# Chunk attention and two MLPs on one core: another order for the attention units, loads and weight pieces of the first stage

## The chip, the cores and the metric

One core of a Trainium2 chip. Its engines run side by side, each through its own list of instructions in order: TensorE (PE; its weight loads are listed as PEld), VectorE (DVE), ScalarE (ACT), GpSimd (POOL) and SyncE (SP). An engine waits for another only through semaphores. SP and POOL issue the DMAs here. The metric is the device time of one execution in microseconds (us); smaller is better.

## The reference

```python
# q, k, v: (4, 8, 576, 64) float32; attention inside chunks of 64 positions
scores = (q_c @ k_c.T) / sqrt(64);  attn = softmax(scores);  out = attn @ v_c
x = out.transpose(0, 2, 1, 3).reshape(2304, 512)
# first MLP:  d_ff 1536
y = ((x @ w_a) * (x @ w_b)) @ w_out
# second MLP: d_ff 2048, g a rational function of h
h = y @ w_in
g = (a0 + a1 h + a2 h^2 + a3 h^3) / (1 + |b0||h| + |b1| h^2 + 1e-6)
return g @ w_out2                               # (2304, 512) float32
```

## The kernel before

**Products.** The large products are made from pairs of fp32r tiles, a high part (`hi`) and the rest (`lo`). `mm3` (lines 250 to 254) adds three products into one bank: weight hi by x hi, weight hi by x lo, weight lo by x hi. So the first product needs the hi parts, the second x lo, the third weight lo.

**Tokens and units.** The 2304 tokens are 18 units of 128. The attention of a unit u is a list of pieces, each named by a letter: `k` and `q` (four transposes on PE into a PSUM tile, then a copy on ACT), `S` (scores: 32 small matmul instructions on PE into the two PSUM banks "a" and "b", then two maxima and two subtractions on DVE), `X` (exp on ACT), `E` (sum, reciprocal, product on DVE), `P` (four transposes on PE, a copy on ACT), `V` (32 small matmul instructions on PE, then two casts to x hi on ACT), `L` (two subtractions on DVE, to x lo). Units 0 to 2 are the first 384 tokens, units 3 to 5 the next 384. The later units are done in pairs (`a_pair`), whose S, V and transposes use the same PSUM tiles. `ps_at`, for k, q and P, has two tiles; "a" and "b" are shared by S and V.

**Weight pieces.** Each 128 x 1024 raw weight tile is made into its hi and lo parts in four pieces (`w_piece`, lines 201 to 236), a `w` in the lists: piece 0 is two ACT instructions, piece 1 writes the hi of the tile before (ACT) and shifts (DVE), piece 2 is one ACT instruction and writes the lo of the tile before (DVE, line 199) and fetches a raw tile into a buffer that is now free, piece 3 is a DVE add (line 234) and a store. So the lo part of tile n is there once piece 2 of tile n + 1 has run. Tiles are numbered in the order a0, b0, a1, b1, ... of the blocks i of the first MLP.

**Start.** The loads are issued in the order of `LOADS`, all on SP's queue. Then `FIRST` writes out by hand the order in which units 0 to 2 and the first 15 weight pieces are issued; `dN` is N idle products of the identity (`warm`), two PE instructions each; `+k5` issues the load of unit 5's k.

**First stage.** `seq` then runs over (i, h), h being the half of 384 tokens: blocks 0 to 3 with h = 0, blocks 0 to 3 with h = 1, then the other blocks with both. `ab_half` makes one 128 x 384 tile of x @ w_a or x @ w_b from 12 products. In its middle and at its end `half()` is called: it brings the weight pieces up to a count (`w_until`), then moves a clock of its own, `now`, on by 0.5 (`tick`) and issues every piece in `todo` whose time has come, by time and then by the order in which it was put in. So a piece with time t is issued after half number n = 2t - 1. This text writes A0 for the tile of block 0 with w_a, B0 with w_b, and so on; A0 to B3 with h = 0 are sixteen halves, and A0 with h = 1, which reads units 3 to 5, begins at t = 8.

```python
for n in range(UH):                                          # units 3, 4, 5
    a_unit(UH + n, 1.0 + 0.5 * n, (0, 0.5, 1.5, 2, 2.5, 4, 5))    # k q S X E P V
FROM, PER, GAP = 5.5, 4.5, 3.0                               # start of the pairs
w_until(min(12 + 2 * n, 32) / 4 if n < 17 else (n + 18) / 4)
```

So units 3, 4 and 5 are half a unit of time apart: k at 1.0, 1.5 and 2.0, S at 2.5, 3.0 and 3.5, E at 3.5, 4.0 and 4.5, P at 5.0, 5.5 and 6.0, V at 6.0, 6.5 and 7.0. The six pairs follow from 5.5, one every 4.5, the last three another 3.0 later. After the last unit of a group of six, `x_second` puts 14 sums, casts and subtractions of x into `todo`. The stages behind (the first MLP on the other tokens by a scheme with fewer products, its second product, the second MLP) are not touched.

Of the kernel before, what the change touches and what calls it, by code (L numbers as in the profile page):

```python
# [20 lines left out]
def chunk_attention_two_mlps(  # L21
# [35 lines left out]
    P = 128  # L57
    B, H, S, D = q.shape
# [16 lines left out]
    UH = GH // P  # L75
    NQ = NT // GT

    FIRST = (  # L80
        "k0 d2 q0 w w S0 w X0 k1 d2 w E0 q1 w S1 X1 P0 w k2 q2 E1 V0 w S2 X2 L0 P1 w +k5 +q5 w V1 d4 E2 w w +v3 +v4 +v5 "
        "L1 d2 P2 d4 w w V2 d4 L2 w w"
    ).split()
    LOADS = "k0 q0 w k1 q1 v0 w k2 q2 v1 w v2 w k3 q3 k4 q4".split()

    AHEAD = 4
    NWP = 12 - AHEAD
# [150 lines left out]
    def w_until(tiles):  # L238

        while n_cv[1] < min(4 * tiles, 4 * n_cv[2]):  # L240
            w_piece()
# [18 lines left out]
    todo = []  # L260
    now = [0.0]

    def later(dt, f):
        todo.append((now[0] + dt, n_todo[0], f))
        n_todo[0] += 1

    n_todo = [0]
# [13 lines left out]
    un = {}  # L281
# [46 lines left out]
    def a_transpose(u, nm):  # L328

        t = raw.pop((nm, u)).rearrange("p (a b) d -> p a (b d)", b=2)  # L330
        pool, tag = (ps_acc, "acc") if u < UH else (ps_at, "at")
        ps = pool.tile([P, HP, P], F32, name="at", tag=tag)
        for hp in range(HP):
            nc.tensor.transpose(ps[:, hp, :], t[:, hp, :], ident)
        o = a_tmp(u, nm + "T") if u < 2 * UH else a_both(u, nm + "T")[:, u % 2]
        nc.scalar.copy(o, ps)
        un[nm + "T", u] = o

    def a_scores(u):

        qT, kT = un.pop(("qT", u)), un.pop(("kT", u))
        ps = [ps_ab.tile([P, HP, CH], F32, name="at", tag=tag) for tag in "ab"]
        for a in range(2):
            for c in range(2):
                for t in range(2):
                    for b in range(2):
                        r, half, cols = (slice(n * CH, (n + 1) * CH) for n in (b, t, c))
                        hp = 2 * a + t  # L350
                        nc.tensor.matmul(
                            ps[b][half, 2 * a + c, :], qT[r, hp, cols], kT[r, hp, cols], start=True, stop=True
                        )
        m = p_e.tile([P, 2, HP], F32, name="m", tag="m")
        e = a_tmp(u, "e").rearrange("p x (y d) -> p (x y) d", d=CH).rearrange("p (b x) d -> p b x d", b=2)
        for b in range(2):
            nc.vector.tensor_reduce(m[:, b], ps[b], AX.X, ALU.max)
        for b in range(2):
            nc.vector.tensor_tensor(
                e[:, b], ps[b], m[:, b].unsqueeze(2).to_broadcast([P, HP, CH]), ALU.subtract  # L360
            )
        un["e", u] = e.rearrange("p b x d -> p (b x) d")

    def a_exp(u):
        nc.scalar.activation(un["e", u], un["e", u], AF.Exp, scale=SCALE)

    def a_soft(u):
        e = un["e", u]
        s = p_e.tile([P, H], F32, name="s", tag="s")
        nc.vector.tensor_reduce(s, e, AX.X, ALU.add)  # L370
        nc.vector.tensor_scalar(s, s, 1e-9, None, ALU.add)
        nc.vector.reciprocal(s, s)
        nc.vector.tensor_tensor(e, e, s.unsqueeze(2).to_broadcast([P, H, CH]), ALU.mult)

    def a_ptrans(u):

        e = un.pop(("e", u)).rearrange("p (a b) d -> p a (b d)", b=2)
        pool, tag = (ps_acc, "acc") if u < UH else (ps_at, "at")
        ps = pool.tile([P, HP, P], F32, name="at", tag=tag)
        for hp in range(HP):  # L380
            nc.tensor.transpose(ps[:, hp, :], e[:, hp, :], ident)
        o = p_t.tile([P, HP, P], F32, name="pT", tag="T")
        nc.scalar.copy(o, ps)
        un["pT", u] = o

    def a_pv(u):

        pT, vv = un.pop(("pT", u)), raw.pop(("v", u))
        ps = []
        for c in range(2):  # L390
            pool, tag = (ps_acc, "acc") if u < UH else (ps_ab, "ab"[c])
            ps.append(pool.tile([P, HP, CH], F32, name="at", tag=tag))
        for hp in range(HP):
            a, t = divmod(hp, 2)
            for c in range(2):
                for h2 in range(2):
                    r, cols, half = (slice(n * CH, (n + 1) * CH) for n in (c, h2, t))
                    nc.tensor.matmul(
                        ps[c][cols, hp, :], vv[r, 2 * hp + h2, :], pT[r, 2 * h2 + a, half], start=True, stop=True
                    )  # L400
        out = [[t[:, :, u * P + c * CH:u * P + (c + 1) * CH] for t in (x_hi, x_lo)] for c in range(2)]
        for c, (hi, lo) in enumerate(out):
            nc.scalar.copy(hi, ps[c])

        def low():
            for c, (hi, lo) in enumerate(out):
                nc.vector.tensor_tensor(lo, ps[c], hi.bitcast(F32), ALU.subtract)

        un["lo", u] = low
# [104 lines left out]
    def x_second(g):  # L514


        x1, x2 = un.pop(("x32", g, 0)), un.pop(("x32", g, 1))
        b11, b21, b12, b22 = x1[:, 0:2], x1[:, 2:4], x2[:, 0:2], x2[:, 2:4]

        def sub(o, x, y):  # L520
            return lambda: nc.vector.tensor_tensor(o, x, y, ALU.subtract)

        h3, l3 = x_hl(g, 3, b22)
        h5, l5 = x_hl(g, 5, b11)
        h7, l7 = x_hl(g, 7, b12)
        h6, l6 = x_hl(g, 6, b11)
        h4, l4 = x_hl(g, 4, b21)
        ops = (
            sub(b11, b12, b11), h3, sub(b12, b22, b12), h5, l3, h7, l5, sub(b11, b22, b11), sub(b21, b21, b11),
            h6, l7, h4, l6, l4,  # L530
        )
        at = 0.5 if g < NQ - 1 else 5.5
        for n, f in enumerate(ops):

            later(at + 0.5 * (n * (9 if g == NQ - 1 else 12) // len(ops)) + (1.5 if g == NQ - 1 and n >= 7 else 0), f)

    def a_unit(u, at, times):


        def piece(dt, *fs):  # L540
            for f in fs:
                todo.append((at + dt, n_todo[0], f))
                n_todo[0] += 1

        k, q, s, x, e, p, v = times
        if ("kT", u) not in un:
            piece(k, lambda: a_transpose(u, "k"))
            piece(q, lambda: a_transpose(u, "q"))
        piece(s, lambda: a_scores(u))
        piece(x, lambda: a_exp(u))  # L550
        piece(e, lambda: a_soft(u))
        piece(p, lambda: a_ptrans(u))
        piece(v, lambda: a_pv(u))
        piece(v + 0.5, lambda: un.pop(("lo", u))())


    ca_t = const.tile([P, 4], F32, name="ca_t")
# [339 lines left out]

    for item in LOADS:
        if item == "w":
# [5 lines left out]

    for item in FIRST:
        if item == "w":
            w_piece()
            continue
        if item[0] == "d":  # L910
            warm(int(item[1:]))
            continue
        if item[0] == "+":
            a_load(int(item[2]), item[1])
            continue
        what, u = item[:-1], int(item[-1])
        if what in "kq":
            a_transpose(u, what)
        else:
            {"S": a_scores, "X": a_exp, "E": a_soft, "P": a_ptrans, "V": a_pv, "L": lambda u: un.pop(("lo", u))()}[  # L920
                what
            ](u)
    nc.sync.dma_start(out=ca_t, in_=ca.unsqueeze(0).to_broadcast([P, 4]))
    nc.sync.dma_start(out=cb_t, in_=cb.unsqueeze(0).to_broadcast([P, 2]))
    for u in (2 * UH, 2 * UH + 1):
# [1 line left out]


    seq = [(i, h) for h in range(2) for i in range(4)] + [(i, h) for i in range(4, F1) for h in range(2)]
    for n in range(UH):  # L930
        a_unit(UH + n, 1.0 + 0.5 * n, (0, 0.5, 1.5, 2, 2.5, 4, 5))
    FROM, PER, GAP = 5.5, 4.5, 3.0
    K_AT, S_AT, X_AT, E_AT, P_AT, V_AT = (0.0, 1.5), 3.5, 4.5, 5.0, 7.0, 8.0

    def a_pair(u, at):
# [16 lines left out]
        piece(V_AT + 1e-7, lambda: a_pv2(u))  # L952

    for m, nm in enumerate("kq"):
        todo.append((3.0 + m / 2, n_todo[0], lambda nm=nm: a_load(2 * UH + 1, nm)))
        n_todo[0] += 1
    for n in range((NQ - 1) * UH):
        a_pair(2 * UH + 2 * n, FROM + PER * n + (GAP if n >= UH else 0))
# [21 lines left out]
    for op in range(12):  # L980
        at = min(END + 2 + 0.5 * (op // 3), 2.0 * len(seq) - 0.5)
# [4 lines left out]
    def half():  # L986


        n = n_half[0]
        n_half[0] += 1  # L990
        w_until(min(12 + 2 * n, 32) / 4 if n < 17 else (n + 18) / 4)
        if n_cv[1] == 32 or n_cv[1] == 4 * len(order1):
            w_flush()
        tick(0.5)
# [17 lines left out]
    for t in range(1, F1):  # L1012

        if t == 1:
            at = [(0, m // 2) for m in range(12)]
        elif t == 2:
            at = [(2, m) for m in (3, 3, 4, 5)] + [(3, m) for m in (0, 1, 2, 3, 3, 4, 5, 6)]
        else:
            at = [(2 * t - 2 + m // 6, FILLS[m % 6]) for m in range(12)]
# [124 lines left out]
```

## Time and profile before

| what | value |
|---|---|
| median of 3 runs | 900.2 us (899.19 to 900.57) |
| profiled execution | 902.0 us |
| its span, first to last instruction | 900.2 us |
| mean granted TensorE clock | 0.996 |
| busy: PE, DVE, ACT, POOL | 879.4, 717.8, 611.3, 64.6 us |

All instruction times below are counted from the start of that span. The profiled execution took 1.8 us more than its span and 1.8 us more than the median of the runs.

### The profile page before, as it was taken

The numbers are of one execution on the slowest core, as the hardware profiler recorded it, in microseconds if no ns is written. First come the engines' busy times: TensorE is split into PE (matmuls) and PEld (weight loads), VectorE is DVE, ScalarE is ACT, GpSimd is POOL, SyncE is SP. The second block draws the span as 40 slices with busy tenths as digits, with TensorE's granted clock in tenths as the row PEclk, the third lists the DMA queues.
The fourth block names the chain that finished last, engine by engine and source line by source line (L and its number), as shares of the span: only waits on it lengthen the run. The fifth ranks groups of instructions, "written<-read, shape, count | busy, mean of one in ns | idle before, by whom it ended". The sixth has DMA issues, their size and how long they took to land.

```text
span 900.2 us, 14700 instructions
## 1 busy us (share of the span) xinstructions
PE 879.4 (98%) x5532; PEld 788.9 (88%) x5532; DVE 717.8 (80%) x1273; ACT 611.3 (68%) x1091; POOL 64.6 (7%) x122
## 2 busy tenths in 40 slices
PE   6989999999999999999999999999999999999998
PEld 5889989999999999888888999888888888888997
DVE  5657797677878875578677599998889988988896
ACT  6768878345455443568777688877677767776775
POOL 0112111111111111100000000000000000000000
PEclk9999999999999999999999999999999999999999
DMA  9989985234243323678777200200020002000100
GB/s 241 275 246 257 254 237 173 79 106 155 100 153 130 133 98 123 205 252 276 258 249 257 94 1 1 82 1 1 1 93 1 1 1 83 0 1 1 48 1 35
DMA packets 107335, 105.82 MB, mean 118 GB/s; under 512 B 61440, under 2 KB 84480, under 8 KB 107264
## 3 DMA queue, kind: packets, MB, share of 16 engines
q1 hardware_dynamic: 99264, 79.71, 30.0%
q0 software_dynamic: 8000, 25.17, 7.4%
q8 instruction: 43, 0.70, 0.3%
q14 instruction: 28, 0.23, 0.1%
HBM read 74.98 MB, written 29.88 MB: 116 GB/s over the span
## 4 chain that ended last, share of the span: by engine, by line
PE 91%; DVE 1%; ACT 1%; DMA 1%; issue 0%; SPq 0%; DVEq 0%; ACTq 0%
PE h L254 7%; PE h L252 7%; PE h L253 7%; PE acc L253 7%; PE acc L254 7%; PE acc L252 7%; PE acc L762 5%; PE acc L765 5%; PE acc L763 5%; PE ab L252 3%; PE y L252 3%; PE y L253 3%; PE y L254 3%; PE ab L254 3%; PE ab L253 3%; PE q L254 2%
## 5 line engine op out<-in xcount | busy, mean ns | idle before, releaser
L254 PE MATMUL h<-y,w_i 128*128 128x512 f32 (+1 forms) x320 | 117.7, 368 | 0.0
L252 PE MATMUL h<-y,w_i 128*128 128x512 f32 (+1 forms) x320 | 117.7, 368 | 0.0
L253 PE MATMUL h<-y,w_i 128*128 128x512 f32 (+1 forms) x320 | 117.6, 368 | 0.0
L820 ACT ACTIVATE a_ring<-h 128x512 f32<-128x512 f32 (+1 forms) x80 | 44.2, 552 | 85.6 <-PE h L254 85.6
L659 ACT COPY s<-y 128x384 f32<-128x384 f32 x72 | 34.5, 481 | 86.1 <-PE y L254 86.0
L762 PE MATMUL acc<-g_hi,w_o 128*128 128x512 f32 (+1 forms) x240 | 87.3, 370 | 2.1 <-ACT g_hi L740 2.1
L763 PE MATMUL acc<-g_hi,w_o 128*128 128x512 f32 (+1 forms) x240 | 87.2, 370 | 0.0
L823 DVE SCALAR_TENSOR_TENSOR u<-u,cb_t,a_ring 128x512 f32<-128x512 f32 (+1 forms) x80 | 55.6, 696 | 29.3 <-ACT u L821 28.7
L253 PE MATMUL acc<-w_o,g_hi 128*128 128x512 f32 x191 | 74.4, 390 | 0.0
L254 PE MATMUL acc<-w_o,g_lo 128*128 128x512 f32 x191 | 74.4, 389 | 0.0
L252 PE MATMUL acc<-w_o,g_hi 128*128 128x512 f32 x191 | 74.3, 389 | 0.0
L252 PEld LDWEIGHTS h<-y,w_i 128*128 128x128 f32 x320 | 60.1, 188 | 8.7
L253 PEld LDWEIGHTS h<-y,w_i 128*128 128x128 f32 x320 | 60.0, 188 | 8.7
L254 PEld LDWEIGHTS h<-y,w_i 128*128 128x128 f32 x320 | 60.1, 188 | 7.4
L742 DVE TENSOR_TENSOR g_lo<-g_raw,g_hi 128x512 fp32r<-128x512 f32 (+1 forms) x60 | 38.0, 636 | 29.6 <-ACT g_hi L740 21.2
L765 PE MATMUL acc<-g_lo,w_o 128*128 128x512 f32 (+1 forms) x240 | 59.8, 371 | 0.0
L822 ACT ACTIVATE t<-h,ca_t 128x512 f32<-128x512 f32 (+1 forms) x80 | 59.1, 738 | 0.0
L833 DVE SCALAR_TENSOR_TENSOR u<-u,r 128x512 f32<-128x512 f32 (+1 forms) x80 | 50.6, 632 | 9.1 <-ACT r L832 9.1
L825 DVE SCALAR_TENSOR_TENSOR t<-t,ca_t,h 128x512 f32<-128x512 f32 (+1 forms) x80 | 55.6, 695 | 2.8
L832 ACT ACTIVATE r<-r,nlsh 128x512 f32<-128x512 f32 (+1 forms) x80 | 54.6, 682 | 2.6
L831 ACT ACTIVATE r<-u,nlsh 128x512 f32<-128x512 f32 (+1 forms) x80 | 55.5, 694 | 0.5
L834 DVE SCALAR_TENSOR_TENSOR t<-t,ca_t,r 128x512 f32<-128x512 f32 (+1 forms) x80 | 55.4, 693 | 0.0
(210 smaller groups left out, 2393.5 us busy)
## 6 DMA issues: line engine op xcount, KB each, us to landing
w_raw<-in_moe_w_out_dram SPq DMA_DIRECT2D x28, 512.0 KB, 4.4
g_d<-g POOLq DMA_DIRECT2D x72, 192.0 KB, 2.5
g_raw<-g_d SPq DMA_DIRECT2D x48, 256.0 KB, 4.3
w_raw<-in_moe_w_in_dram SPq DMA_DIRECT2D x16, 512.0 KB, 4.6
w_raw<-in_moe_w_a_dram SPq DMA_DIRECT2D x12, 512.0 KB, 5.3
w_raw<-in_moe_w_b_dram SPq DMA_DIRECT2D x12, 512.0 KB, 4.9
out_dram<-o SPq DMA_DIRECT2D x18, 256.0 KB, 2.4
y_d<-ys POOLq DMA_DIRECT2D x16, 256.0 KB, 4.4
```

The source lines that it names most:

```text
L252: nc.tensor.matmul(ps, wh, xh, start=first, stop=False, **kw)
L253: nc.tensor.matmul(ps, wh, xl, start=False, stop=False, **kw)
L254: nc.tensor.matmul(ps, wl, xh, start=False, stop=last, **kw)
L762: nc.tensor.matmul(acc[j][d], wh, gh, start=i == 0, stop=False)
L763: nc.tensor.matmul(acc[j][d], wl, gh, start=False, stop=False)
L765: nc.tensor.matmul(acc[j][d], cols(w, d)[0], gl, start=False, stop=i == F1 - 1)
L822: nc.scalar.activation(t, ps, AF.Identity, scale=ca_t[:, 3:4], bias=ca_t[:, 2:3])
L823: nc.vector.scalar_tensor_tensor(u, u, cb_t[:, 0:1], ah, ALU.add, ALU.mult)
L825: nc.vector.scalar_tensor_tensor(t, t, ca_t[:, 1:2], ps, ALU.add, ALU.mult)
L831: nc.scalar.activation(r, u, AF.Ln, scale=2.0 ** -LSH, bias=nlsh[:, 0:1])
L832: nc.scalar.activation(r, r, AF.Exp, scale=-1.0, bias=nlsh[:, 1:2])
L834: nc.vector.scalar_tensor_tensor(t, t, ca_t[:, 0:1], r, ALU.add, ALU.mult)
```

## The change

Nothing is added to or taken from the computation. The order in which it is issued changes in these places: in `LOADS` weight tile b0 goes ahead of v0 and b1 ahead of v2; in `FIRST` the idle products are put elsewhere (16 for 18), some weight pieces stand one place earlier or later and the loads of v3, v4, q5 and v5 go around weight tile 6's fetch; units 3 to 5 get a table of times of their own, in which unit 4 (the fifth) goes in front of unit 3; the count of weight pieces is one lower until it reaches 32; the last three pairs start 0.5 earlier; and the sums of x of a group start 0.5 earlier, the first group's spread over 13 places for 12.

```diff
-    FIRST = (
-        "k0 d2 q0 w w S0 w X0 k1 d2 w E0 q1 w S1 X1 P0 w k2 q2 E1 V0 w S2 X2 L0 P1 w +k5 +q5 w V1 d4 E2 w w +v3 +v4 +v5 "
-        "L1 d2 P2 d4 w w V2 d4 L2 w w"
-    ).split()
-    LOADS = "k0 q0 w k1 q1 v0 w k2 q2 v1 w v2 w k3 q3 k4 q4".split()
+    FIRST = "k0 q0 w w d2 S0 w X0 w k1 E0 d2 q1 S1 w X1 P0 k2 w q2 E1 V0 w S2 X2 L0 w d2 P1 w V1 d4 +k5 E2 +v4 +q5 +v3 w w L1 P2 d2 +v5 w V2 d4 w L2 w w".split()
+    LOADS = "k0 q0 w k1 q1 w v0 k2 q2 v1 w w v2 k3 q3 k4 q4".split()
...
-        at = 0.5 if g < NQ - 1 else 5.5
+        at = 0.0 if g < NQ - 1 else 5.0
...
-            later(at + 0.5 * (n * (9 if g == NQ - 1 else 12) // len(ops)) + (1.5 if g == NQ - 1 and n >= 7 else 0), f)
+            later(at + 0.5 * (n * (9 if g == NQ - 1 else 13) // len(ops)) + (1.5 if g == NQ - 1 and n >= 7 else 0), f)
...
-        k, q, s, x, e, p, v = times
-        if ("kT", u) not in un:
-            piece(k, lambda: a_transpose(u, "k"))
-            piece(q, lambda: a_transpose(u, "q"))
-        piece(s, lambda: a_scores(u))
-        piece(x, lambda: a_exp(u))
-        piece(e, lambda: a_soft(u))
-        piece(p, lambda: a_ptrans(u))
-        piece(v, lambda: a_pv(u))
-        piece(v + 0.5, lambda: un.pop(("lo", u))())
+        for what, dt in zip("kqSXEPVL", times):
+            if f"{what}{u}" not in FIRST:
+                piece(dt, lambda what=what: a_piece(what, u))
...
-    for n in range(UH):
-        a_unit(UH + n, 1.0 + 0.5 * n, (0, 0.5, 1.5, 2, 2.5, 4, 5))
-    FROM, PER, GAP = 5.5, 4.5, 3.0
+    UNITS = (
+        (1.0, 2.0, 3.0, 3.5, 4.0, 5.5, 6.5, 6.5),
+        (0.5, 0.5, 1.0, 1.5, 2.0, 3.5, 4.5, 5.0),
+        (3.0, 3.0, 3.5, 4.0, 5.5, 6.5, 7.5, 7.5),
+    )
+    for n, times in enumerate(UNITS):
+        a_unit(UH + n, 0.0, times)
+    FROM, PER, GAP = 5.5, 4.5, 2.5
...
-        todo.append((3.0 + m / 2, n_todo[0], lambda nm=nm: a_load(2 * UH + 1, nm)))
+        todo.append((2.5 + m / 2, n_todo[0], lambda nm=nm: a_load(2 * UH + 1, nm)))
...
-        w_until(min(12 + 2 * n, 32) / 4 if n < 17 else (n + 18) / 4)
+        w_until(min(11 + 2 * n, 32) / 4 if n < 17 else (n + 18) / 4)
```

The new function `a_piece(what, u)` holds the branch over the letters that stood in the loop over `FIRST`. The three rows of `UNITS` are the times of units 3, 4 and 5 in the order k, q, S, X, E, P, V, L.

## Rows read from the trace of the kernel before

**Rows 1.** The page: PE's busy tenths, 40 equal slices of the span.

```profile
PE   6989999999999999999999999999999999999998
```

**Rows 2.** Windows of 25 us: busy of each engine, clock, DMA share, GB/s.

```profile
25.00:50.00 25.00, 21.25 (x205) 19.19 (x206) 17.74 (x42) 18.40 (x34) 3.79 (x7) 0.93 1.02 277
```

**Rows 3.** PE's waits, 0 to 200: who for whom, us in total, times, longest.

```profile
PE ab L254 <- DVE w_b L199: 2.6, 1, 2.6
...
PE at L474 <- ACT qT L336: 0.4, 1, 0.4
```

**Rows 4.** Timeline of SP's queue: start us, us, instruction.

```profile
2.64 0.51 SPq L325 DMA_DIRECT2D kqv<-in_k_dram  x1
...
26.55 3.48 SPq L172 DMA_DIRECT2D w_raw<-in_moe_w_a_dram  x1
```

**Rows 5.** Those two DMAs: KB, us from issue to landing.

```profile
kqv<-in_k_dram SPq DMA_DIRECT2D x1, 256.0 KB, 5.8
...
w_raw<-in_moe_w_a_dram SPq DMA_DIRECT2D x1, 512.0 KB, 8.5
```

**Rows 6.** Timeline 8 to 28: start us, us, engine and line, [idle before].

```profile
8.49 1.11 PE L334 MATMUL at<-ident,kqv 128*128 128x128 f32 x4
...
21.42 1.60 PE L895 MATMUL at<-ident 128*128 128x128 f32 x12
...
23.50 0.59 ACT L383 COPY pT<-at 128x512 f32<-128x512 f32 x1
...
24.29 0.69 PE L398 MATMUL at<-pT,kqv 64*64 64x64 f32 x32
...
25.18 0.65 ACT L403 CAST x_hi<-at 128x256 fp32r<-128x256 f32 x2
...
25.88 0.44 PE L252 MATMUL ab<-x_hi,w_a 128*128 128x384 f32 x1
...
26.39 0.44 PE L253 MATMUL ab<-x_lo,w_a 128*128 128x384 f32 x1
```

**Rows 7.** Timeline of DVE, 40 to 48: the first instruction of each piece.

```profile
40.82 0.68 DVE L370 TENSOR_REDUCE s<-e 128x8 f32<-128x512 f32 x1
...
42.59 0.75 DVE L357 TENSOR_REDUCE m<-at 128x4 f32<-128x256 f32 x2
...
43.92 0.55 DVE L577 TENSOR_TENSOR g<-ab,a_s 128x384 f32<-128x384 f32 x1
...
44.38 0.42 DVE L224 TENSOR_SCALAR w_a<-w_a 128x512 int32<-128x512 int32 x1
...
44.71 0.68 DVE L370 TENSOR_REDUCE s<-e 128x8 f32<-128x512 f32 x1
...
46.48 0.69 DVE L199 TENSOR_TENSOR w_b<-w_x,w_b 128x512 fp32r<-128x512 f32 x1
47.08 0.68 DVE L234 CUSTOM_DVE_ANT_0 w_x<-w_a 128x1024 uint16<-128x1024 uint16 x1
```

**Rows 8.** Timeline of PE, 33 to 60.

```profile
33.86 0.69 PE L351 MATMUL at<-kT,qT 64*64 64x64 f32 x32
34.49 0.66 PE L334 MATMUL at<-ident,kqv 128*128 128x128 f32 x4
...
44.31 0.34 PE L253 MATMUL ab<-x_lo,w_b 128*128 128x384 f32 x1
...
47.22 0.69 PE L254 MATMUL ab<-x_hi,w_b 128*128 128x384 f32 x1 [2.57 <-DVE w_b L199]
...
58.50 0.60 PE L334 MATMUL at<-ident,kq 128*128 128x128 f32 x4
58.85 0.42 PE L252 MATMUL ab<-x_hi,w_b 128*128 128x384 f32 x1
...
59.98 0.33 PE L252 MATMUL ab<-x_hi,w_a 128*128 128x384 f32 x1
```

**Rows 9.** Windows of 0.5 us, the same columns as rows 2.

```profile
47.00:47.50 0.50, 0.28 (x1) 0.28 (x2) 0.50 (x2) 0.00 (x0) 0.00 (x0) 0.50 0.77 231
```

More of the change, by code (lines that the diff above doesn't have):

```diff
@@ L531, in x_second, with a_piece @@
         )
-        at = 0.5 if g < NQ - 1 else 5.5
+        at = 0.0 if g < NQ - 1 else 5.0
         for n, f in enumerate(ops):
-            later(at + 0.5 * (n * (9 if g == NQ - 1 else 12) // len(ops)) + (1.5 if g == NQ - 1 and n >= 7 else 0), f)
+            later(at + 0.5 * (n * (9 if g == NQ - 1 else 13) // len(ops)) + (1.5 if g == NQ - 1 and n >= 7 else 0), f)
+    def a_piece(what, u):
+        if what in "kq":
+            a_transpose(u, what)
+        else:
+            {"S": a_scores, "X": a_exp, "E": a_soft, "P": a_ptrans, "V": a_pv, "L": lambda u: un.pop(("lo", u))()}[
+                what
+            ](u)
     def a_unit(u, at, times):
@@ L915, in chunk_attention_two_mlps @@
             continue
[L916 to L922, printed above, removed]
+        a_piece(item[:-1], int(item[-1]))
     nc.sync.dma_start(out=ca_t, in_=ca.unsqueeze(0).to_broadcast([P, 4]))
```

## The prediction, made before the changed kernel ran

> **What bounds the kernel now.** I read the page's slices first [rows 1]: PE is busy in every slice but the first (6 tenths) and the third (8). Behind the first stage its list is full, so a reorder there could win almost nothing, and what is won before that reaches the end. Second, the 25 us windows [rows 2]: from 25 to 50 PE is busy for 21.25 of 25 us at a mean clock of 0.93, so this is where time lies. Third, PE's waits [rows 3]: the longest is 2.6 us, for the lo part of a weight tile (line 199). Fourth, the timelines. The first product of A0 starts at 25.88 [rows 6], the first of A0 with h = 1 at 59.98 [rows 8]: 34.1 us. What is PE's own work in between?
>
> - 16 halves of six products. 58.85 to 59.98 [rows 8] is one such half: 1.13 each, 18.1.
> - 13 groups of four transposes (k, q, P of units 3 to 5; k and q of units 6 and 7). 58.50 to 58.85: 0.35 each, 4.55.
> - 3 S and 3 V, 32 instructions of one size each. 33.86 to 34.49: 0.63 each, 3.8, and 0.1 apiece for getting in, an estimate of mine: 0.6.
>
> That is 27.0 us. So 7.1 of the 34.1 are waits and a slow clock. The largest: B2's third product should follow 0.2 us behind the second (44.31), and starts at 47.22 [rows 8], 2.7 late. In the idle time the granted clock falls to 0.50 [rows 9], the 1.2 GHz level; the mean of 0.93 over 25 us [rows 2] means 3.5 us at it. Some 0.5 of them are idle, so 3.0 us at half rate cost 1.5 more. The other 2.9 are shorter waits.
>
> Why was that lo part late? It is a piece on DVE, which ran without a gap [rows 7]: E of unit 3 (1.77 us from 40.82), the DVE part of S of unit 5 (1.33), a product, a shift, E of unit 4 (1.77), and only then, at 46.48, line 199. Three units half a time apart put their S and E in one bunch, in front of the weight pieces.
>
> **The change, part by part.**
>
> *Start: 0.3 us gained, not more.* The loads bound it at first. The k load of unit 1, issued at 2.64 [rows 4], lands 5.8 us later [rows 5], at 8.44, and its transposes start at 8.49 [rows 6]. Up to there the order of loads doesn't change. S0 can go a little earlier, but k1, d2, q1 and S1 follow as now, and from S1 to V1 the new order issues the same things to ACT and DVE. b0 ahead of v0 and b1 ahead of v2 put a v load behind 512 KB, 1.9 us at the 277 GB/s of rows 2. I count that at nothing, since V0 and V2 stand at the end of their units' chains; without that cover V2 would be at most 1.9 later. The gain is at the end. Today 12 PE instructions of idle products (1.60 us from 21.42) stand ahead of P2, and two more d4 around V2. Now 8 are ahead of P2, and 4 ahead of V2. P2's copy (ACT, 23.50, 0.59 long) is bound by ACT's own list and stays; V2, at 24.29 today, starts when it ends, at 24.1. V2 and 8 idle instructions take 1.6 us (24.29 to 25.88), so A0 starts at 25.7. The casts of V2, which today start at 25.18 behind piece 0 of tile 3, now stand ahead of it, and start when V2 is done, 24.85. That is 0.33 earlier, so A0's second product, which waits for x lo, starts at 26.05 for 26.39 [rows 6].
>
> *Units 3 to 5: 5.5 us gained.* I walk the new list with the same prices. PE: 26.05, the rest of the half to 27.0, k4 and q4, a half, k3, S4 and two halves, with B0's result at 32.4. DVE takes B0's product (0.46) and then, piece by piece by the starts in rows 7 (E 1.77; S 1.33; shift 0.33; lo part 0.60; piece 3 is as long and gets 0.60): piece 3 of tile 3, E4, shift, lo of tile 3, piece 3 of tile 4, S3, ending at 38.1. S5 is next on PE by 32.2 + 0.35 + 2 x 1.13 + 0.73 + 0.70 + 1.13 + 0.35 = 37.7. It needs bank "b", which S3's last subtraction frees: **a wait of 0.4**. DVE goes on: shift, lo of tile 4, S5, product, piece 3, E3, shift; 0.33 + 0.60 + 1.33 + 0.46 + 0.60 + 1.77 + 0.33 = 5.4, so the lo of tile 5 runs from 43.5 to 44.2. PE is at B2's third product by 37.7 + 0.4 + 0.73 + 3 x 1.13 + 0.73 + 0.45 = 43.4, and 0.1 for each of two groups: **a wait of 0.7**, where now it is 2.7. I take it that a wait a quarter as long as today's leaves the clock alone. What is late next? P3, k6, q6, V3, P5, k7, V5, q7 find their inputs: carried on like this, E5 ends at 48.2 and P5 comes at 49; V5's lo parts end at about 54.0, and A0 with h = 1 wants them at 54.1. So: 25.7 + 27.0 + 0.33 (x lo of unit 2, as now) + 0.4 + 0.7 = 54.1, against 59.98. This and the start are 5.8 together.
>
> ACT is taken to keep up: busy 18.40 of 25 us [rows 2]. Where it doesn't (its order puts hi parts, copies and exps behind pieces 0 and 2), what is late is the lo part of tile 5, by up to 1 to 2 us.
>
> *The weight count one lower* puts tile 5's lo in the same half as before, its hi one later. That is in the walk. *The loads of v4, v3 ahead of tile 6's raw tile:* that lands at 26.55 + 8.5 = 35.1 now [rows 4, 5]. Two loads of 256 KB at 277 GB/s [rows 2] make it 37.0. ACT's list has it behind P4's copy and X3, which follows S3's end at 38.1, so not before 39: I count nothing, with 2 us to spare.
>
> The Trainium skill ("DMA: Bandwidth & Descriptors", Specifications) wants at least 512 B per transfer for the full rate; k, q and v are read in runs of 64 floats, 256 B. If each such load cost what a 512 KB weight tile costs, tile 6 would land at 38.9: the sum stays, with nothing to spare. No row here times such a load against a weight tile alone. By that rule the rival of a late load, below, is likelier than by the row.
>
> *The later pairs, 0.5 earlier: 0.4.* V of the third pair now comes in the same tick as a q that must be copied out of the same PSUM tiles first, and waits 0.4 for it [rows 3]. With 2.5 for 3.0 that q is half a unit ahead. The sums of x half a time earlier and over 13 places: DVE gets the same instructions in the same order; no price that I can find, bounds -0.5 to +1.0 (twice the wait of 0.4, or the 0.4 and a little gone).
>
> Sum: 5.8 + 0.4 = 6.2. The profiled execution's 902.0 would be 895.8; it stands 1.8 above the median, so 900.2 becomes **894.0**. 0.2% is 1.8 us, about what a measurement here can tell from no change.
>
> **The rivals.**
>
> *The wait at tile 5 stays long.* For: the vector queue has no gap there, any 1 us more (a late exp, a late hi part) is 1 us of PE. If it is 2.7 us as today, it costs 2.0 more and the clock's 1.5: 897.5. Against: in the walk one E, not two, stands right in front of it. Chance 0.18.
>
> *A load is late.* Tile 6 lands after 39; ACT stands, and with it the hi of tile 5. 1.5 us past that is 1.5, with 0.7 there already: 895.5, and 897 once the clock falls. Chance 0.08.
>
> *The loads set the pace of the whole stage.* DMA's share is 1.02 at 277 GB/s from 25 to 50 [rows 2]; if PE only ever follows the loads, the order of units moves nothing but the 0.3 of the start: 899.9. Against: PE's longest wait names DVE [rows 3], whose list had no gap [rows 7]. Chance 0.09.
>
> *Slower: unit 5's sums.* V5 and L5 stand at 7.5, one half in front of A0 with h = 1, which reads them; before, V5 stood one half earlier still. The walk leaves no slack. Each us by which L5 is late is a us of PE, and in a wait like today's at B2 the clock adds 1.5. From 4.7 us late (6.2 less 1.5) it is even, and 8 us late gives 903.5. For: E5, the last one, now waits until 5.5. Against: DVE and ACT have no bunch left there. Chance 0.07.
>
> **How the numbers follow.** The forecast has 0.58, its own range 892.2 to 895.8 (the waits of 0.4 and 0.7 gone, 0.5 at the later pairs and 0.2 of rounding, or 1.0 at the later pairs and 0.8 by ACT). The long wait 0.18, a late load 0.08, loads as the pace 0.09, slower 0.07. Faster by over 0.2%: 0.58 + 0.18 + 0.08 = 0.84; within 0.2%: 0.09; slower: 0.07. The range is 892.2 to 898.0: it takes in the first two rivals' times, and leaves out the last two and the edges, some 2 in 10.
>
> **What would show it.** A0's first product at 25.7 and its second at 26.05 (start). A0 with h = 1 at about 54 (units). The wait for line 199 at B2 under 1 us, and no window near 44 to 50 with a clock under 1.00. A wait of 0.4 at S5 for DVE. No wait at line 474 for a q copy near 100. The rows of waits would prove me wrong with a line on kqv or w_raw (loads), on x_lo at line 407 around 54 (unit 5), or a wait of over 2 us for line 199 and a low clock behind it. The prediction fails above all where ACT, which I only bounded, is late.

## The result and the profile after

The changed kernel takes 891.73 us in the median of 4 runs (891.41 to 893.33), the kernel before 900.37 (899.19 to 900.57). The ratio is 0.9905, with a 95% interval of 0.9892 to 0.9919: 8.6 us faster. The forecast was 894.0 with a range of 892.2 to 898.0, so the sign was right and the gain was larger than the range allowed, by half a us. The profiled execution took 891.73 us with a span of 890.0, 10.2 less than the span before.

The page's slices of the kernel after, the row that answers to [rows 1]:

```profile
PE   6999999999999999999999999999999999999998
```

The third slice, 8 before, is now 9. The 25 us window of [rows 2], busy of PE, PEld, DVE, ACT and POOL, then clock, DMA share and GB/s:

```profile
25.00:50.00 25.00, 24.15 (x290) 21.84 (x290) 19.92 (x47) 20.65 (x40) 4.72 (x9) 1.00 1.02 282
```

PE is busy for 24.15 us of 25 (21.25 before), at a clock of 1.00 (0.93 before). The waits of PE up to 200, for [rows 3]; who waited for whom, us in total, times, longest:

```profile
PE at L395 <- ACT pT L380: 2.2, 3, 1.6
...
PE ab L251 <- DVE w_b L196: 0.8, 1, 0.8
PE at L331 <- ACT pT L380: 0.6, 1, 0.6
PE at L457 <- DVE e L450: 0.3, 1, 0.3
PE at L471 <- ACT pT L458: 0.2, 1, 0.2
```

The line numbers are 3 lower than before: L251 is `mm3`'s third product, L331 the transposes, L395 V, L457 and L471 the pairs' P and V. The wait for a weight's lo part at B2 is 0.8 for 2.6. The pairs' waits of 0.8, 0.4 and 0.4 are 0.3 and 0.2, and the 0.4 for a weight sum at the start of the next stage is gone. The timeline of PE, where the start ends and where the second half begins, for [rows 6] and [rows 8]; start us, us, engine and line:

```profile
25.69 0.44 PE L250 MATMUL ab<-x_lo,w_a 128*128 128x384 f32 x1
```

```profile
42.99 0.34 PE L250 MATMUL ab<-x_lo,w_b 128*128 128x384 f32 x1
44.14 0.45 PE L251 MATMUL ab<-x_hi,w_b 128*128 128x384 f32 x1 [0.81 <-DVE w_b L196]
...
51.35 0.63 PE L331 MATMUL at<-ident,kq 128*128 128x128 f32 x4 [0.56 <-ACT pT L380]
...
55.14 0.33 PE L249 MATMUL ab<-x_hi,w_a 128*128 128x384 f32 x1
```

A0's second product is at 25.69 (26.39 before), B2's third 1.15 behind its second (2.9 before), A0 with h = 1 at 55.14 (59.98 before). The row at 51.35 is new: k7 waits. The row names the copy of P5 on ACT, which ended at 51.35, 0.1 us behind the landing of k7's own load (issued at 44.93, 6.3 us to landing). The DVE list ahead of B2, for [rows 7]:

```profile
41.30 0.67 DVE L367 TENSOR_REDUCE s<-e 128x8 f32<-128x512 f32 x1
...
43.40 0.69 DVE L196 TENSOR_TENSOR w_b<-w_x,w_b 128x512 fp32r<-128x512 f32 x1
```

E3 (from 41.30), the shift and the lo of tile 5 run one after the other, the lo part from 43.40 to 44.09. The walk of the prediction had it from 43.5 to 44.2.

To compare all kernels I cut each profiled execution at four instructions of PE's timeline: A0's second product, A0's first with h = 1, the first product of the next stage, the last of that stage; then the end of the span. The lengths in us, with the wait for g at the seam behind the fourth cut and the clock from 20 to 30 us:

| kernel | to A0's 2nd | 16 halves | rest of first stage | next stage | to the end | wait at seam | clock 20 to 30 |
|---|---|---|---|---|---|---|---|
| before | 26.39 | 33.59 | 115.16 | 176.91 | 548.15 | 2.1 | 1.00 |
| after | 25.69 | 29.45 | 113.51 | 176.03 | 545.32 | 0.7 | 1.00 |
| e1 start only | 25.80 | 34.52 | 115.16 | 176.91 | 545.91 | 1.4 | 1.00 |
| e2 units only | 28.93 | 28.67 | 115.15 | 176.91 | 545.04 | 0.8 | 0.67 |
| e3 pairs only | 27.53 | 33.72 | 113.49 | 176.04 | 544.92 | 0.7 | 0.83 |
| e4 after, seam | 24.81 | 30.27 | 113.50 | 176.04 | 543.98 | none | 1.00 |
| e5 GAP only | 27.42 | 33.60 | 113.59 | 176.07 | 547.92 | 1.9 | 0.83 |
| e6 sums only | 26.93 | 33.59 | 114.46 | 176.07 | 545.95 | 1.2 | 0.83 |
| e7 after, no d2 | 26.66 | 29.76 | 113.49 | 176.04 | 544.85 | 0.6 | 0.83 |
| e8 three more | 25.18 | 28.98 | 114.70 | 176.04 | 544.00 | none | 1.00 |
| e9 units 3, 4 exchanged | 25.78 | 29.19 | 113.49 | 176.04 | 545.50 | 1.3 | 1.00 |
| e10 count 12 | 24.93 | 31.77 | 113.49 | 176.04 | 545.87 | 1.6 | 1.00 |
| e11 v late | 25.36 | 28.66 | 113.48 | 176.05 | 545.75 | 1.5 | 1.00 |
| e12 v late, seam | 25.36 | 28.66 | 113.48 | 176.04 | 543.96 | none | 1.00 |

Between the two profiled executions that makes 0.7 + 4.1 + 1.65 + 0.9 + 2.8 = 10.2 us. The fourth column takes two values and the third four (115.2, 113.5, and 114.5 and 114.7 in e6 and e8): what a part does there repeats to 0.1 us. The first column and the seam move from execution to execution, and the halves move too: the kernel after and e4, which are the same up to the seam, have 29.45 and 30.27, with a wait of 0.6 and of 1.4 at k7.

### The profile page after: what moved, and what is told of

Its sections match the earlier page's. It is cut to its first block, busy times and chain, and to the rows that moved or that the text cites. A ratio compares the mean times of both kernels' runs of the same rounds, so it can differ in the third digit from the quotient of the medians.

```text
span 890.0 us, 14694 instructions
## 1 busy us (share of the span) xinstructions
PE 873.8 (98%) x5528; PEld 783.7 (88%) x5528; DVE 717.4 (81%) x1273; ACT 610.5 (69%) x1091; POOL 64.4 (7%) x122
## 4 chain that ended last, share of the span: by engine, by line
PE 92%; ACT 1%; DVE 1%; DMA 1%; issue 0%; SPq 0%; ACTq 0%; DVEq 0%
PE h L249 7%; PE h L251 7%; PE h L250 7%; PE acc L251 7%; PE acc L249 7%; PE acc L250 7%; PE acc L761 5%; PE acc L762 5%; PE acc L764 5%; PE ab L249 3%; PE ab L251 3%; PE ab L250 3%; PE y L249 3%; PE y L250 3%; PE y L251 3%; PE q L249 2%
## 5 line engine op out<-in xcount | busy, mean ns | idle before, releaser
L251 PE MATMUL h<-y,w_i 128*128 128x512 f32 (+1 forms) x320 | 117.7, 368 | 0.0
L251 PE MATMUL acc<-w_o,g_lo 128*128 128x512 f32 x191 | 74.4, 389 | 0.0
L251 PEld LDWEIGHTS h<-y,w_i 128*128 128x128 f32 x320 | 60.1, 188 | 7.5
```

Source lines behind the costliest of these rows:

```text
L251: nc.tensor.matmul(ps, wl, xh, start=False, stop=last, **kw)
```

## The experiments

**The parts alone: e1, e2, e3.** e1 is the kernel before with the new `LOADS` and `FIRST`. e2 is the kernel before with the new times of units 3 to 5 and the count of 11:

```diff
+    UNITS = ((1.0, 2.0, 3.0, ...), (0.5, 0.5, 1.0, ...), (3.0, 3.0, 3.5, ...))
-        w_until(min(12 + 2 * n, 32) / 4 ...
+        w_until(min(11 + 2 * n, 32) / 4 ...
```

e3 is the kernel before with

```diff
-    FROM, PER, GAP = 5.5, 4.5, 3.0
+    FROM, PER, GAP = 5.5, 4.5, 2.5
-        todo.append((3.0 + m / 2, ...
+        todo.append((2.5 + m / 2, ...
-        at = 0.5 if g < NQ - 1 else 5.5
+        at = 0.0 if g < NQ - 1 else 5.0
...
-            later(at + 0.5 * (n * (9 if g == NQ - 1 else 12) // len(ops)) + ...
+            later(at + 0.5 * (n * (9 if g == NQ - 1 else 13) // len(ops)) + ...
```

that is the later pairs, the loads of k7 and q7, and the sums of x. (`...` marks what is left out of a line or between lines.)

> The kernel before with the new LOADS and FIRST alone (units 3 to 5, the weight count and the pairs as before). Theory A, each part wins in its own stage and the parts add: the second product of A0 at 25.7 to 26.05 for 26.39, so 0.3 to 0.7 us less than before, 899.7 to 900.1; the wait for line 199 at B2 and the slow clock behind it stay (2.5 us or more). Rival B, the start and the units only work together (the late wait at B2 takes back what the start wins): no change, 900.4. Rival C, the early rise of PE's speed (S1 in 0.8 us for 1.2) came by chance: A0's second product at 26.05.

> The kernel after with LOADS, FIRST and the later pairs put back: only the times of units 3 to 5 and the weight count of 11 are new. Theory A: 4.1 us less in the sixteen halves, 896.2, with a wait of about 0.8 for the lo part at B2 and one of about 0.6 at k7. Rival B: more than 5 us less, since the start adds nothing of its own, or less than 3 because v3, v4, v5 come in the old order. The waits from 95 to 130 (0.4, 0.4, 0.8) stay.

> The kernel before with GAP 2.5, the two loads at 2.5 and the sums of x half a unit earlier (13 places), nothing else. Theory A: the waits of 0.4, 0.4 and 0.8 from 95 to 130 and the one of 0.4 at 183 shrink, 2.0 to 2.5 us less, 898. Rival D, as the prediction had it: only the 0.4 before V of the third pair goes, 900.0. Rival E: no gain alone, since the pairs' waits shrank because all of the stage ran earlier against the loads: 900.4.

Ratios to the kernel before: e1 0.9990 (0.9981 to 0.9999, 899.83 us), e2 0.9952 (0.9934 to 0.9969, 896.00 us), e3 0.9962 (0.9948 to 0.9975, 897.48 us). Their product is 0.9904, and the whole change has 0.9905: within these intervals the parts add (theory A). In the table e2 acts on the halves, 4.9 us there, and e3 on the two columns behind, 2.5 us. So the pairs' part, priced at 0.4 in the prediction, is worth 2.5, and rivals D and E fall. The wait that was expected at k7 in e2 didn't come: its halves begin 3.2 us later than those of the kernel after, and the load is there in time.

e1 is nearer to rival B in its profile. It won 0.6 in the start and lost 0.9 in the halves: PE's waits between 29 and 55 us add up to 5.9 us for 3.8 in the kernel before, the largest of them, beside B2's 2.6, 1.3 at S5 (0.4 before) and 1.0 at P5 (0.2 before). What PE gains at the start is lost there as long as the old bunch stands behind it. The slow clock that was expected behind B2's wait did not come in this execution; the clock is 1.00 from 40 to 60 us.

In the start, e2 and e3 show what the profile of before didn't. A window of 10 us of e2:

```profile
20.00:30.00 10.00, 9.24 (x103) 8.66 (x104) 6.50 (x15) 7.39 (x15) 1.08 (x2) 0.67 1.03 254
```

Behind a wait of PE of 2.1 us at V1 the clock is 0.67 over 20 to 30, much of it at the level of 0.50, and A0's second product is at 28.93 for 26.39. The wait is there in the execution of before too, without the fall.

**e7, the kernel after without one pair of idle products.** The pair of idle products (`d2`, four PE instructions) ahead of P1 shortens that wait.

```diff
-  ... L0 w d2 P1 w V1 ...
+  ... L0 w P1 w V1 ...
```

> The kernel after without the one idle product pair (d2, four PE instructions) ahead of P1. Theory J, this pair shortens PE's wait at V1 (1.6 for 2.1 us) and so keeps the clock up: without it the wait is 2.1 again and in some executions the clock falls to 0.50 between 20 and 28, A0's second product then at 27 to 29 for 25.7, and the median is 0.5 to 1.5 us above the kernel after. Rival K, the pair only fills idle time: the same as the kernel after, 891.7, and the falls seen with the old start came from its other differences.

```profile
PE at L395 <- ACT pT L380: 2.1, 1, 2.1
```

```profile
20.00:30.00 10.00, 9.58 (x112) 8.81 (x112) 6.12 (x14) 7.98 (x17) 1.08 (x2) 0.83 0.89 241
```

The wait is 2.1 again (1.6 in the kernel after), the clock falls to 0.83 over those 10 us and A0's second product moves from 25.69 to 26.66 (from V1 to there it is 6.5 us for 5.3). The median is 892.86, the ratio to the kernel before 0.9914 (0.9900 to 0.9928). The time alone doesn't tell it from the kernel after, the profile does. Over all profiled executions: with the wait at 2.0 or 2.1 (before, e2, e3, e5, e6, e7) the clock fell between 20 and 30 in five of six; with 1.5 or 1.6 (the other eight) in none. Five of those six have the old start, so e7 alone separates the pair from the rest of it. The mean clock of the whole span, which is on record for every run though it doesn't say where a fall lies, points the same way: 0.998 in five of e7's six runs, and 0.998 or less in five of the 30 runs of the seven kernels that have the new start with the pair and the new units. So rival K falls for the wait and the clock, as theory J has it; the median that J expected, 0.5 to 1.5 us higher, stays within the noise.

**e5 and e6: the pairs' part in two.** e5 has only `GAP` at 2.5, e6 only the sums of x earlier and over 13 places.

> The kernel before with GAP 2.5 for 3.0 and nothing else. The pairs' part alone won 2.5 us between A0 with h = 1 and the end of the first MLP's first products. Theory H, the place of the last three pairs makes all of it: the waits at 104, 123.6 and 126.1 shrink and the one of 0.4 for a weight sum at 183 goes too (the next stage's preparation starts half a unit sooner): 2.5 us in these two stretches. Rival I, the prediction's: only the 0.4 at the third pair's V; the rest is the sums' part (next run).

> The kernel before with the sums of x half a unit earlier and over 13 places, GAP as before. Theory H: nothing by itself, 0 to 0.4 us in the two stretches. Rival I: the sums stand less in the way of E of the fourth pair on DVE, the waits of 0.4 and 0.8 near 123 to 126 go, 1.5 to 2 us.

e5: 0.9966 (0.9952 to 0.9980, 898.06 us); e6: 0.9984 (0.9974 to 0.9995, 899.10 us). In the two columns e5 wins 1.6 + 0.8 and e6 0.7 + 0.8, and both together with the two loads (e3) 1.7 + 0.9, so what they win is in large part the same. PE's waits from 85 to 130 in e5 and in e6 (0.8, 0.4 and 0.4 in the kernel before):

```profile
PE at L460 <- ACT w_a L219: 0.4, 1, 0.4
PE at L474 <- ACT pT L461: 0.2, 1, 0.2
```

```profile
PE at L460 <- ACT qT L336: 0.7, 1, 0.7
PE at L474 <- ACT qT L336: 0.4, 1, 0.4
```

`GAP` alone makes nearly all of it (theory H), but H is wrong on the sums: alone, earlier sums take the wait of P for E (0.4) away, as rival I had it in kind, and leave that of V. The wait of 0.4 for a weight sum, at 184.6 in the kernel before, goes with either.

**e9 and e10: unit order and weight count.** e9 is the kernel after with the rows of units 3 and 4 in `UNITS` exchanged; e10 has `min(12 + 2 * n, 32)` again.

> The kernel after with the time tables of units 3 and 4 exchanged, so that unit 3 goes first and unit 5 last; loads as in the kernel after. Theory L, it is the spread of the three units over time that wins in the sixteen halves, not which unit goes first: the same as the kernel after, 891.7 (within 1 us), wait of 0.8 at B2 again. Rival M, the order matters (unit 4 first frees buffers or meets its loads better): over 1 us slower than the kernel after.

> The kernel after with the weight count of the kernel before (12 for 11 pieces ahead). Theory: the hi of tile 5 comes one half earlier, its lo in the same half, so the wait at B2 is as it was, 0.8, and the time the same to 0.5 us. Rival: one piece more in front of E4 and S3 delays the attention pieces on DVE, other waits of 0.5 to 1.5 us in the sixteen halves, 892.5 to 893.

e9: 891.89 us, 0.9905 (0.9888 to 0.9922), the halves 29.19: the same as the kernel after. Which unit goes first makes no difference that these runs show; what is left of e2's edit is the spread over time (theory L) and the count. e10: 893.05 us, 0.9917 (0.9902 to 0.9932); its interval overlaps that of the kernel after. Its one profile has 31.77 in the halves, with a wait at q6 (at 48.91) and waits of 1.2 in all for the loads of two other q's that the kernel after doesn't have, and 0.5 at B2 for 0.8. The first of them:

```profile
PE at L331 <- ACT pT L380: 1.5, 1, 1.5
```

That execution was 0.8 early in its first column, so the loads may account for a part. What the count of 11 is worth stays open between 0 and 1.3 us.

**e11: the load behind the wait at k7.** The v of units 6 and 7 is loaded at 7.0 and not in front of tile 8 and k7.

```diff
-        a_load(u, "k", "q", "v") if u == 2 * UH else a_load(u, "v")
+        if u == 2 * UH:
+            a_load(u, "k", "q")
+        todo.append((7.0, n_todo[0], lambda u=u: a_load(u, "v")))
+        n_todo[0] += 1
```

> The kernel after with the loads of v of units 6 and 7 (512 KB, wanted only at 13.5) issued at 7.0, not ahead of tile 8 and of k and q of units 7 and 8. Theory N, since the start is earlier the loads bind at k7: its load lands 2 us sooner, the wait of 0.6 to 1.4 at k7 goes, 0.6 to 1 us less than the kernel after, 891. Rival O, k7 waits for the copy of P5 on ACT (as the row of waits names it): no change, 891.7.

891.04 us, 0.9895 (0.9881 to 0.9910). PE's waits from 24 to 60 are one line:

```profile
PE ab L251 <- DVE w_b L196: 0.8, 1, 0.8
```

The wait at k7 is gone and the halves take 28.66 for 29.45 (theory N), in e12 again, and in e2, whose halves begin late, 28.67. It was k7's load; rival O, what the row named, falls. In e4, e7 and e9 the same row names the DMA. The time alone doesn't show it: the interval overlaps that of the kernel after.

**e4, e8, e12: the seam, and a faster version.** e4 is the kernel after with `w2_begin()` at `n == 6` for `n == 3`, so that two weight loads of 512 KB no longer stand in front of g's load. e8 adds the load of k7 and q7 at 2.0 and E of unit 3 at 4.5. e12 is e11 and e4.

> The kernel after, with the two first loads of the second MLP's weights (512 KB each) issued three steps later in the second product of the first MLP (at step 6 for 3). Theory F, the wait for g at the seam (0.7 us after, 2.1 and a slow clock before) comes from g's load standing behind and beside those two loads: the wait is gone, 0.7 to 1.2 us less than the kernel after, 890.5 to 891. Rival G, the wait is the round trip of g through memory: no change, 891.7; or it moves to where the weights are wanted, and the time is longer than 891.7.

> The kernel after with three more edits: the loads of unit 7's k and q at 2.0 (ahead of tile 8's fetch), E of unit 3 at 4.5 for 4.0 (behind the lo part of tile 5), and the two weight loads at the seam three steps later. Theory: the waits of 0.6 to 1.4 at k7, of 0.8 at B2 and of 0.7 at the seam go: 2 us less than the kernel after, 889.5. Rival: the load of tile 8 or E of unit 3 is late in turn (P3 waits), and no more than 0.5 us is won.

> e11 and the two weight loads at the seam three steps later (as in e4), together. Theory: no wait at k7 and none at the seam: 1.3 to 2 us less than the kernel after, 890. Rival: what is won at k7 is lost at k8 or q8, whose loads come behind, as with e8: 891.

The wait behind the seam in the kernel after and in e11, from PE's waits of 300 to 420:

```profile
PE acc L761 <- ACT g_hi L739: 0.7, 1, 0.7
```

```profile
PE acc L761 <- ACT g_hi L739: 1.5, 1, 1.5
```

e4, e8 and e12 have no row there, and 1.3 to 1.8 us less in the last column than the executions with the loads at step 3 and the same kernel otherwise (after and e4, e11 and e12). So theory F holds. The wait was 0.6 to 2.1 in the eleven others and goes with no part of the change. e4: 891.22 us, 0.9895 (0.9878 to 0.9911). e8: 891.16 us, 0.9893 (0.9878 to 0.9908); its rival was right in kind:

```profile
PE at L331 <- DMA k<-in_k_dram: 1.0, 1, 1.0
PE at L378 <- DVE e L370: 0.6, 1, 0.6
```

With k7's load ahead, k8's is late by 1.0 (most of the 1.2 that e8 loses in the third column), and with E3 behind the lo part of tile 5, P3 waits 0.6 for it. e12: 890.01 us, 0.9883 (0.9869 to 0.9898), the fastest version here, 10.5 us under the kernel before; its interval still meets that of the kernel after at the edge, and those of e4 and e8 overlap it.

## Why the prediction was wrong

**Where the time lies** was right: the first stage, B2's wait and the slow clock behind it.

**The units** were walked nearly as they ran: the lo of tile 5 at 43.40 (43.5 foretold), B2's wait 0.8 (0.7), S5 at 37.87 (37.7) and the half behind it at 38.73 (38.8). The wait of 0.4 at S5 has no row of its own; S5 took 0.93 us for the 0.69 of S3. The term was 5.5 and came to 4.1 in the kernel after, 4.9 in e2 and e11: k7's load wasn't in the walk, 0.8 us at that place, and the other 0.6 isn't located. The rival of a late load was right in kind and named the wrong load: tile 6 landed at 37.7, 1.7 ahead of its first ACT instruction at 39.40. The sum by bytes had 37.0 for that landing. The prediction also weighed the rule of the Trainium skill ("DMA: Bandwidth & Descriptors", Specifications) that the full rate wants at least 512 B per transfer, at a price of its own, each such load costing what a 512 KB weight tile costs: 38.9. The measured 37.7 lies between the two, nearer to the bytes, so that price isn't borne out here. Windows with one kind of transfer agree: where every packet was under 512 B (23.6 to 24.4 us) the kernel after moved 224 GB/s and the one before 263; where nearly all were larger (26 to 28) they moved 289 and 357. By these a byte of k, q or v took 1.3 to 1.4 times as long, an estimate, and not twice.

**The start** was given 0.3 "and not more". The profiled execution shows 0.7. Of it 0.4 lies between V1 and A0's second product (5.7 us before, 5.3 in all eight executions with the pair ahead of P1): that is the term. The other 0.3 lies ahead of V1, whose start moves by 1.0 us between executions with either start, so it isn't shown to be the change's. S1 ran at the full clock (0.79 us for 1.23), but so it did in three of the five executions with the old start (e3, e5, e6); rival C of e1 isn't ruled out. What the term left out is the idle pair ahead of P1, which the prediction took for one of "the same things": it keeps the clock up in the wait at V1 (e7). The profile of before, from which the prediction was worked out, had no fall there to show it.

**The step that failed is "The later pairs, 0.5 earlier: 0.4."** Its mechanism was right for V of the third pair, but its size was 2.5 (e3, and the two columns of the kernel after), outside the 0.9 that the range allowed it (0.4, and 0.5 more). The waits of 0.8 and 0.4 at the fourth pair's P, and the 0.4 for a weight sum in the next stage, stood in the same view as the one that was counted, and no row was taken for them:

```profile
PE at L460 <- ACT qT L336: 0.8, 1, 0.8
PE q L254 <- DVE j_x L631: 0.4, 1, 0.4
...
PE at L460 <- DVE e L453: 0.4, 1, 0.4
```

They fall with the same edit (0.3 and 0.2 are left in the kernel after); `GAP` also brings the preparation of the next stage half a unit forward (`END` is worked out from it), but through which piece each wait goes isn't shown. With 2.5 for 0.4 the sum would have been 8.3 us, 891.9 from 900.2. That this is near the measured 891.73 is luck: the units were 1.4 too high in it, and what the idle pair saves wasn't in it.

**The seam** was not named. It gave 2.8 of the 10.2 us between the two profiles, and it is not the change's: its wait is 0.6 to 2.1 in any kernel with the loads at step 3. In the execution of before the wait was 2.1 (0.7 in the one of after), and behind it the granted clock was 0.52 and 0.62 in the two windows of 2 us from 364 to 368 us. That this execution stood 1.8 above its median, and the one of after on its median, fits with that.

The rivals: a long wait at tile 5, loads as the pace and unit 5's sums didn't come. The sums of unit 5 end at 54.86 and A0 with h = 1 starts at 55.14 without a wait.

## What to carry to other kernels

Before a shift of work in time is priced, list every wait in the stretch where the shifted pieces meet others, and ask of each whether the shift changes that meeting. A term with "no price that I can find" should get the sum of those waits as its first size. It is no limit: here the rows add up to 2.0 us, 0.5 of them stayed, and 2.5 were won. A second: cut the trace at a few fixed instructions and compare stretch by stretch. A difference in a stretch that repeats to 0.1 us between executions can be put down to the change; one in a stretch that moves from run to run can't, from one profile.

## What the runs showed of the hardware

Behind PE's wait of 2.0 to 2.1 us at V1 the granted clock fell to the 0.50 level in five of six executions; behind 1.5 or 1.6 us, with the idle pair ahead of P1, in none of eight. At B2 a wait of 0.5 to 0.8 left the clock at 1.00, and one of 2.5 to 2.6 took it to 0.50 in four of five (before [rows 9], e3, e5 and e6; not in e1). At the seam it fell behind 1.9 and 2.1 us (e5, before) and not behind 0.6 to 1.6 in the nine others that have a wait there. So the same wait can leave the clock alone in one execution and not in the next. e5 and e11 also show a fall between 14 and 18 us, which no run explains.

The fall at V1 is best priced from V1's first product to A0's second, since V1 itself moves by 1.0 between executions: with the old start 5.7 us in the execution before (20.70 to 26.39, no fall), 7.2 in e3 (20.36 to 27.53) and e6 (19.76 to 26.93), 7.3 in e5 (20.09 to 27.42), 8.2 in e2 (20.76 to 28.93); with the new start 5.3 in the kernel after (20.39 to 25.69) and 6.5 in e7 (20.20 to 26.66). So it cost 1.2 to 2.5 us, and a single profile can miss it, as that of the kernel before did.
